# The first pair's maxima in another order, its small work moved to GpSimd, fillers that go on until the first score, and a re-planned order

## The chip, the cores and the metric

The kernel runs on one core of a Trainium2 chip. The metric is device microseconds of one execution; a lower time is better. One execution is also recorded by the hardware profiler, and the rows below come from that one. Engines are named as in the profile: PE (matmuls), PEld (its weight loads), DVE (VectorE), ACT (ScalarE), POOL (GpSimd) and SP (the queue that issues most transfers).

## The reference

Pooled attention, then a feed-forward layer with a two-slope activation:

```python
q_pool = q.reshape(B, H, S // 2, 2, D).mean(axis=3)       # B 4, H 8, S 1152, D 64
scores = (1 / sqrt(D)) * q_pool @ k.T
scores = scores - scores.max(axis=-1)
attn = exp(scores) / (exp(scores).sum(axis=-1) + 1e-9)
x = (attn @ v)  # laid out as 2304 tokens x 512
h = x @ w_in                                              # 512 -> 2048
y = (max(h, 0) + alpha * min(h, 0)) @ w_out               # 2048 -> 512
```

The scores need more precision than one float32r product gives, so q and k are each split into a high part (a rounded copy, `q1`, `k1`) and a low part (the rest, `q2`, `k2`), and a score is the sum of three products. The weights come as 64-bit floats and are converted and split on the core.

## The kernel before, in words

The 32 heads are worked in 16 **pairs**; a pair's two heads sit in the two 64-row halves of PE, and two matmuls on different halves can run side by side. For a pair there are 576 pooled queries and 1152 keys.

- **Maxima.** Before the scores, each query's maximum is found from a rough product of the high parts (lines 815 and 822, one matmul of 384 columns per query tile, third of the keys and head; 28 results a pair, the last 64 queries apart as "rests"). DVE reduces each from its PSUM bank to one column of `bx` (line 836). The columns are then turned into a row `mq`. For pairs 1 to 15 that is one turn (lines 845, 852) and small transfers; for the first pair it is two turns (`first_turn`, lines 892, 904, 915, 921).
- **Scores.** A group of eight matmuls (line 948) makes the scores of 128 keys for half of the queries (288), for both heads: the last two subtract `mq`. ACT takes the exponential into a tile `pa` (line 964). There are 9 groups in a half of a pair, so 18 groups in a pair.
- **Sums over keys.** The `pa` tiles of a half are added up to two partial sums (line 977), seven adds in a half, some on DVE and some on POOL (the table `ADDS`). PE adds up the partitions (line 1013), four matmuls for each partial sum. Weighted values come from 18 matmuls at the end of a half (line 991).
- **Feed-forward.** The first 5 of 16 blocks of the hidden layer are done in "low sweeps", the rest in "high sweeps" after attention (line 477). The weights' conversion (lines 404 to 425 and 386, 389) goes in between on ACT and DVE.

The order on each engine is written by a planner: a list scheduler (`Scheduler`) has a duration, a priority and the buffers of each task and places tasks as its plan says; each engine then runs its list in that order, and waits where an input is late. `lock=True` marks tasks that the planner keeps from overlapping between DVE and POOL. Parameters such as `TO_PE`, `M0` or `W0` shift priorities and assumed delays.

At the start `warm` issues filler matmuls (line 1123) on two otherwise unused banks, while loads and the first reduces go on. `first_prep` loads the first pair in pieces, sums the two halves of each query pair (line 740), and makes the low parts (lines 770 and 781).

Of the kernel before, what the change touches and what calls it, by code (L numbers as in the profile page):

```python
# [225 lines left out]
def attention_ffn(  # L226
# [11 lines left out]
    DF: int = 1843,  # L238
    D0: int = 1153.836,
    AQ: int = 0,  # L240
    F0: float = 6.733,
    F2: float = 0.839,
    FD: tuple = (0, 0, 0),
    WE: float = 13.725,
    WG: int = 1,
    WT: float = 9.076,
    WM: int = 2,
    WB: int = 300,
    WN: int = 4,
    TO_PE: int = 127,  # L250
    FROM_PE: int = 0,
    SLP: int = 47,
    SLA: int = 48,
    SLD: int = 108,
    QL: float = -0.025,
    KL: float = 1.207,
    KR: float = 1.483,
    KS: float = 0.198,
    M0: float = 0.994,
# [7 lines left out]
    KKB: int = 2,  # L267
    SF: int = -39,
    Q0: float = -3.222,
# [5 lines left out]
    ADDS: tuple = ((4, 6, 8), (6, 7, 8)),  # L275
# [5 lines left out]
    R0: float = 6.346,  # L281
    R1: float = -5.36,
    R2: float = -5.985,
    R3: float = -0.231,
    W0: float = 5.682,
    W1: float = 3.256,
    W2: float = 23.45,
    W3: float = 0.87,
# [5 lines left out]
    GL: float = 21.701,  # L294
    COL: float = 0.135,
    HW: float = -1.196,
# [407 lines left out]
    first_load = [None]  # L704

    def first_prep():
# [4 lines left out]
        qc = (slice(0, 2 * P), slice(2 * P, 3 * P), slice(3 * P, SQ))  # L711
# [24 lines left out]
        for i, c in enumerate(qc):  # L736
            m = c.stop - c.start
            q_sum.append(add(
                DVE, dve(m),
                lambda c=c: nc.vector.tensor_tensor(  # L740
# [19 lines left out]
            ACT, act(D), lambda: nc.scalar.activation(out=w.rt.t[:, D:2 * D], in_=qs.t[:, REM:], func=AF.Copy),  # L760
            uses=[qs], deps=[q_sum[2]], writes=[w.rt], prio=-8.3,
# [27 lines left out]
    def pair_max(n, w):  # L789
# [11 lines left out]
        items[BD:BD] = rests  # L801
        if first:
            items = [(t, j) for t in range(NQT - 1) for j in range(NJ)] + rests
        items = [(t, j, i) for t, j in items for i in range(2)]
        for x, (t, j, i) in enumerate(items):
# [7 lines left out]
            def rows(t=t, j=j, d=d, ms=ms):  # L813
                if t >= 0:
                    nc.tensor.matmul(  # L815
                        out=ms.t[:, :JW], lhsT=w.q1.t[d, t * P:(t + 1) * P],
                        rhs=w.k1.t[d, j * JW:(j + 1) * JW], start=True, stop=True,
                    )
                    return
# [7 lines left out]
            dur = 140 if rest else 95  # L827
            if first:
                deps = w.k_in if rest else [w.k_in[j], w.q_in[(0, 0, 1, 2)[t]]]
# [9 lines left out]
            if first and x in (6 * NJ - 1, len(items) - 1):  # L839
                first_turn(x > 6 * NJ, w, bx, mx, mq)  # L840
# [43 lines left out]
    def first_turn(h, w, bx, mx, mq):  # L884
        ts = ((0, 1, 2), (3, -1))[h]
        p = -8.8 + 0.1 * h
        m = Buf(r_one)

        def peak(lo, n):
            return add(  # L890
                DVE, 90,
                lambda: nc.vector.tensor_reduce(
                    out=mx.t[:, lo:lo + n], in_=bx.t[:, lo:lo + n], axis=AX.X, op=ALU.max
                ),
                reads=[bx], deps=list(mx.writers), writes=[mx], prio=p,
            )

        done = [peak(2, 3), peak(6, 3)] if not h else [peak(0, 2 * NQT)]

        def turn():  # L900
            for x, t in enumerate(ts):
                for i in range(2):
                    col = i if t < 0 else 2 + t + i * (NQT - 1)
                    nc.tensor.matmul(
                        out=m.t[i * D:i * D + 1, x * P:(x + 1) * P], lhsT=mx.t[:, col:col + 1].bitcast(F32),
# [3 lines left out]
        add(PE, 110 * 2 * len(ts), turn, deps=done, uses=[mx], writes=[m], prio=p, kind="s", col=2)  # L909
        for i in range(2):  # L910
            o = slice(i * D, i * D + 1)
            lo, hi = (0, 3 * P) if not h else (3 * P, 4 * P)
            w.mq_in[h].append(add(
                ACT, act(hi - lo, True),
                lambda o=o, lo=lo, hi=hi: nc.scalar.activation(out=mq.t[o, lo:hi], in_=m.t[o, :hi - lo], func=AF.Copy),
                reads=[m], writes=[mq], prio=p + 0.01 * i,
            ))
            if h:
# [3 lines left out]
                        out=mq.t[o, REM:], in_=m.t[o, P:2 * P].rearrange("o (i q) -> o q i", q=D), axis=AX.X, op=ALU.max  # L922
# [305 lines left out]
```

## Time and profile before

| | us |
|---|---|
| median of 3 runs | 849.56 (849.19 to 850.66) |
| the profiled execution | 848.91 |
| its span, first to last instruction | 847.1 |
| PE busy in it | 833.1 (98%) |
| DVE busy | 574.5 (68%) |
| ACT busy | 436.4 (52%) |
| POOL busy | 207.3 (24%) |

The profiled execution is 0.65 us under the median, and 1.8 us of it lie outside the span. A busy PE is not PE at its peak: matmuls are pipelined, their ends are modelled, and two halves can run side by side or not. Shares over the whole span mix a stage with attention (to about 430 us) and one of feed-forward alone.

### The profile page before, as it was taken

Reading aid. Unit: us, or ns where it says so; the run is one execution under the profiler, and the core shown is the slowest. Engines: PE = TensorE matmul, PEld = TensorE weight load, DVE = VectorE, ACT = ScalarE, POOL = GpSimd, SP = SyncE. Lnnn points to the kernel's source line nnn. Section 1 sums busy time; section 2 is a strip of 40 time slices with the busy share of each in tenths; the row PEclk is TensorE's granted clock in tenths of the full one; section 3 lists DMA queues with packets and bytes.
Section 4 is the critical chain, followed back from the end, with each engine's and each line's share of the span. In section 5 each row is a group of like instructions: output and inputs, shape, how many; then the busy total and the mean of one; then the engine's idle time right before and its main releaser. Section 6 shows DMA issues by size and latency. Waiting matters only on the chain.

```text
span 847.1 us, 17444 instructions
## 1 busy us (share of the span) xinstructions
PE 833.1 (98%) x6686; PEld 695.8 (82%) x6686; DVE 574.5 (68%) x1071; ACT 436.4 (52%) x1124; POOL 207.3 (24%) x159
## 2 busy tenths in 40 slices
PE   9999999999999999999899999999999999999997
PEld 7776766777777777777679999998888988988986
DVE  7899999999999989888864689733232332322422
ACT  3575756766766766765764567543232143232321
POOL 2353644545555435554420000000000000000000
PEclk9799999999999999999999999999999999999999
DMA  6333444542445433323333766573330321200301
GB/s 218 89 82 114 134 114 127 190 138 76 125 150 143 125 99 87 89 69 99 127 104 110 238 221 224 195 217 88 90 90 0 104 76 45 82 9 1 90 1 45
DMA packets 67759, 93.71 MB, mean 111 GB/s; under 512 B 20004, under 2 KB 45404, under 8 KB 67676
## 3 DMA queue, kind: packets, MB, share of 16 engines
q1 hardware_dynamic: 65516, 88.18, 33.6%
q0 software_dynamic: 2160, 4.42, 3.6%
q8 instruction: 52, 0.85, 0.4%
q14 instruction: 31, 0.25, 0.1%
HBM read 73.48 MB, written 19.02 MB: 109 GB/s over the span
## 4 chain that ended last, share of the span: by engine, by line
PE 88%; DVE 5%; DMA 2%; issue 2%; ACT 2%; SPq 0%; DVEq 0%; ACTq 0%
PE bank L477 43%; PE bank L948 18%; PE bank L991 14%; PE bank L815 6%; PE bank L1013 2%; PE bank L1123 2%; PE bank L822 2%; DMA wraw<-wt 1%; DVE pa L977 1%; DVE bx L836 1%; DVE wbits L413 1%; DMA x<-xs 1%; DVE pos L513 0%; DVE wmag L425 0%; ACT neg L508 0%
## 5 line engine op out<-in xcount | busy, mean ns | idle before, releaser
L977 POOL TENSOR_TENSOR pa<-pa,pa 128x576 f32<-128x576 f32 x128 | 190.6, 1511 | 207.8 <-ACT pa L964 196.5
L836 DVE TENSOR_REDUCE bx<-bank 128x1 f32<-128x384 f32 (+1 forms) x448 | 216.0, 537 | 20.8 <-PE bank L815 14.8
L964 ACT ACTIVATE pa<-bank 128x288 f32<-128x288 f32 x576 | 196.7, 415 | 33.3 <-PE bank L948 23.1
L948 PE MATMUL bank<-q,k 64*128 64x288 f32 x1728 | 207.6, 314 | 0.2
L948 PEld LDWEIGHTS bank<-q,k 64*128 64x128 f32 x1728 | 162.7, 187 | 12.8 <-issue 4.4
L991 PE MATMUL bank<-pa,vv 128*64 128x288 f32 x1152 | 146.8, 409 | 0.0
L991 PEld LDWEIGHTS bank<-pa,vv 128*64 128x64 f32 x1152 | 79.9, 137 | 56.2 <-issue 5.5
L524 DVE TENSOR_TENSOR gw<-gs,gw 128x460 fp32r<-128x460 f32 (+1 forms) x55 | 35.1, 639 | 121.2 <-ACT gw L519 121.2
L948 PE MATMUL bank<-mq,neg 64*128 64x288 f32 x576 | 114.3, 293 | 0.0
L815 PE MATMUL bank<-k,q 64*128 64x384 f32 x384 | 109.4, 366 | 1.9 <-DVE bx L836 1.6
L519 ACT ACTIVATE gw<-gs 128x460 fp32r<-128x460 f32 (+1 forms) x55 | 32.4, 589 | 126.7 <-PE bank L477 115.2
L477 PE MATMUL bank<-wlow,wh 128*128 128x460 f32 (+1 forms) x320 | 92.9, 371 | 0.0
L477 PE MATMUL bank<-gw,wh 128*128 128x460 f32 (+1 forms) x320 | 92.8, 371 | 0.0
L977 DVE TENSOR_TENSOR pa<-pa,pa 128x576 f32<-128x576 f32 x96 | 84.0, 875 | 0.2
L948 PEld LDWEIGHTS bank<-mq,neg 64*128 64x128 f32 x576 | 82.6, 187 | 0.0
L815 PEld LDWEIGHTS bank<-k,q 64*128 64x128 f32 x384 | 62.3, 185 | 16.5 <-DVE bx L836 10.1
L513 DVE SCALAR_TENSOR_TENSOR gs<-gs,nal 128x460 f32<-128x460 f32 (+1 forms) x55 | 38.5, 699 | 52.8 <-ACT gs L508 52.8
L477 PE MATMUL bank<-x,wlow 128*128 128x288 f32 x480 | 66.5, 296 | 0.0
L477 PE MATMUL bank<-gs,wlow 128*128 128x288 f32 x480 | 65.5, 295 | 0.8 <-DVE gs L524 0.7
L477 PEld LDWEIGHTS bank<-wlow,wh 128*128 128x128 f32 x320 | 60.1, 188 | 7.1
L477 PEld LDWEIGHTS bank<-gw,wh 128*128 128x128 f32 x320 | 60.1, 188 | 6.8
L477 PEld LDWEIGHTS bank<-gs,wlow 128*128 128x128 f32 x480 | 63.9, 188 | 1.9 <-DVE gs L524 1.4
(89 smaller groups left out, 996.7 us busy)
## 6 DMA issues: line engine op xcount, KB each, us to landing
wraw<-wt SPq DMA_DIRECT2D x32, 512.0 KB
vv<-vt SPq DMA_DIRECT2D x32, 288.0 KB
xs<-x SPq DMA_DIRECT2D x32, 288.0 KB
x<-xs SPq DMA_DIRECT2D x32, 288.0 KB
kk<-kt SPq DMA_DIRECT2D x15, 576.0 KB
r<-rrd SPq DMA_DIRECT2D x64, 72.0 KB
yp<-ys SPq DMA_DIRECT2D x32, 144.0 KB
wlow<-xs SPq DMA_DIRECT2D x16, 288.0 KB
```

The costliest lines, as they stand in the source:

```text
L477: nc.tensor.matmul(out=ps[:, :n], lhsT=w[a, c // DMO][:, c % DMO:c % DMO + P], rhs=lo(hl), start=(first and i == 0), stop=(last and i == 2),)
L513: lambda: nc.vector.scalar_tensor_tensor(out=flat(pos), in0=flat(neg), scalar=nal[:, f:f + 1], in1=flat(pos), op0=ALU.mult, op1=ALU.add),
L519: ACT, act(n), lambda: nc.scalar.activation(out=gs.t[:, 0, :n], in_=flat(pos), func=AF.Copy),
L524: lambda: nc.vector.tensor_tensor(out=gs.t[:, 1, :n], in0=flat(pos), in1=gs.t[:, 0, :n].bitcast(F32), op=ALU.subtract),
L815: nc.tensor.matmul(out=ms.t[:, :JW], lhsT=w.q1.t[d, t * P:(t + 1) * P], rhs=w.k1.t[d, j * JW:(j + 1) * JW], start=True, stop=True,)
L822: nc.tensor.matmul(out=ms.t[:, :S // 4], lhsT=w.rt.t[d, D - D * u:D - D * u + P], rhs=w.k1.t[d, c:c + S // 4], start=u == 0, stop=u == 1,)
L836: nc.vector.tensor_reduce(out=bx.t[:, at, j:j + 1], in_=ms.t[:, :m], axis=AX.X, op=ALU.max)
L948: nc.tensor.matmul(out=ps.t[i][:, :HQ], lhsT=k.t[d, s] if k else neg[d], rhs=r.t[d, q], start=x == 0, stop=x == len(pairs) - 1,)
L964: lambda ps=ps, p=p, i=i: nc.scalar.activation(out=p.t[:, i], in_=ps.t[i][:, :HQ], func=AF.Exp, scale=SCALE),
L977: lambda a=a, b=p, part=part, e=e: e.tensor_tensor(out=part.t, in0=a.t, in1=b.t, op=ALU.add),
L991: nc.tensor.matmul(out=av.t[i * D:(i + 1) * D, :HQ], lhsT=w.vv[i].t[:, e], rhs=p.t[:, i], start=(e == 0), stop=(e == NC - 1),)
L1013: nc.tensor.matmul(out=ps.t[g * 32:(g + 1) * 32, :HQ], lhsT=ones, rhs=acc[n + g // 2][j].t[:, g % 2], start=j == 0, stop=j == m - 1, tile_ ...
```

## The change

Code: (1) The first pair's maxima come in the order: query tiles 0 and 1, the rests, tiles 2 and 3. For the first pair the rests are queries 256 to 319, so that the first turn covers queries 0 to 319, and so all 288 queries of its first half. (2) `first_turn` takes its bank from the score banks (`r_ps`) in place of bank 0, which the maxima now share from the start. (3) Two of the three query sums, and the three low-part subtractions of the first pair, go to POOL (`FQ`, `FD`). (4) Fillers are planned until the first score group is placed (or 24 us), have 256 columns throughout, and use banks 1 and 7. (5) The planner's assumed times of a maxima matmul (95 to 130 ns, rests 140 to 190 ns), a score group (540 to 545 ns) and a filler are longer. (6) In each half of a pair the add of key tile 7 moves from DVE to POOL (`ADDS`), 32 adds in all. (7) Some 30 priorities and delays of the plan have other values, which moves instructions everywhere.

```diff
-    FD: tuple = (0, 0, 0),
+    FD: tuple = (1, 1, 1),
-    WE: float = 13.725,
+    WE: float = 24.0,
-    WN: int = 4,
+    WN: int = 2,
+    FQ: int = 1,
+    FB: tuple = (1, 7),
-    ADDS: tuple = ((4, 6, 8), (6, 7, 8)),
+    ADDS: tuple = ((4, 6, 8), (6, 8)),
...
-        qc = (slice(0, 2 * P), slice(2 * P, 3 * P), slice(3 * P, SQ))
+        qc = (slice(0, 2 * P), slice(2 * P, 2 * P + D), slice(2 * P + D, SQ))
...
+            eng1, dur, e1 = pair_op(i and FQ, m)
             q_sum.append(add(
-                DVE, dve(m),
-                lambda c=c: nc.vector.tensor_tensor(
+                eng1, dur,
+                lambda c=c, e1=e1: e1.tensor_tensor(
...
-        items[BD:BD] = rests
-        if first:
-            items = [(t, j) for t in range(NQT - 1) for j in range(NJ)] + rests
+        at = 2 * NJ if first else BD
+        items[at:at] = rests
+        starts = [t * P + D * (first and t > 1) for t in range(NQT - 1)]
...
-            dur = 140 if rest else 95
+            dur = 190 if rest else 130
...
-            if first and x in (6 * NJ - 1, len(items) - 1):
-                first_turn(x > 6 * NJ, w, bx, mx, mq)
+            if first and x in (4 * NJ + 3, len(items) - 1):
+                first_turn(x > 4 * NJ + 3, w, bx, mx, mq)
...
-        m = Buf(r_one)
+        m = Buf(r_ps)
...
-        done = [peak(2, 3), peak(6, 3)] if not h else [peak(0, 2 * NQT)]
+        done = [peak(4, 6), peak(8, 10)] if h else [peak(0, 4), peak(6, 8)]
...
-        filler = [Buf(r_av), Buf(r_one)]
+        filler = [Buf(Banks()), Buf(Banks())]
+        for f, i in zip(filler, FB):
+            f.ring.places = [single[i]]
...
-            if sch.now < WE * 1000:
-                add_warm()
+            add_warm()
 
         def add_warm():
-            if not WE:
+            if first_score and first_score[0].end is not None or sch.now > WE * 1000:
                 return
-            n = WN if sch.now < WT * 1000 else WM
-            add(PE, 58 * n, lambda: warm(n), writes=filler, prio=50, kind="warm", col=1)
+            cold = sch.now < WT * 1000
+            n = WN if cold else WM
+            add(PE, (107 if cold else 58) * n, lambda: warm(n), writes=filler, prio=50, kind="warm", col=1)
```

The new file has six more lines, so that its line numbers are 2 to 6 higher (815 becomes 818, 836 becomes 839, 892 becomes 894, 904 becomes 906, 948 becomes 951, 977 becomes 981).

**Place one: PE, from the last maxima of the first pair to its first score.** Before (`k_189`, `q_185` are the first pair's, `k_362`, `q_368` the second's; `rt` holds the rests):

```order
L815 MATMUL bank_118<-k_189,q_185 128x384
L815 MATMUL bank_124<-k_189,q_185 128x384
L822 MATMUL bank_123<-k_189,rt_109 128x288 x2
L822 MATMUL bank_118<-k_189,rt_109 128x288 x2
L822 MATMUL bank_124<-k_189,rt_109 128x288 x2
L822 MATMUL bank_123<-k_189,rt_109 128x288 x2
L904 MATMUL bank_118<-ident,mx_107 1x128 x6
L815 MATMUL bank_124<-k_362,q_368 128x384
L815 MATMUL bank_123<-k_362,q_368 128x384
L904 MATMUL bank_118<-ident,mx_107 1x128 x4
L948 MATMUL bank_119<-q_185,k_189 128x288
L948 MATMUL bank_120<-q_185,k_189 128x288
```

In the changed kernel, at the same place (`k_191`, `q_187` are the first pair's; 1129 is the filler's line):

```order
L818 MATMUL bank_123<-k_191,q_187 128x384
L906 MATMUL bank_120<-ident,mx_107 1x128 x6
L818 MATMUL bank_124<-k_191,q_187 128x384
L818 MATMUL bank_118<-k_191,q_187 128x384
L1129 MATMUL bank_119<-even 128x256
L1129 MATMUL bank_125<-even 128x256
L818 MATMUL bank_123<-k_191,q_187 128x384
L1129 MATMUL bank_119<-even 128x256
L1129 MATMUL bank_125<-even 128x256
L1129 MATMUL bank_119<-even 128x256
L1129 MATMUL bank_125<-even 128x256
L951 MATMUL bank_120<-q_187,k_191 128x288
```

Before, all 28 results of the first pair and both turns stand ahead of the first score. Now 21 of the 28 stand ahead of the first turn and 24 ahead of the first score; the second turn follows four score groups and three maxima of the second pair later. In front of the first maxima matmul stand 36 fillers of 512 columns before, and 38 of 256 columns now.

**Place two: DVE and POOL in the first pair.** DVE before, from the first pair's last reduce on (770 and 781 are the low parts, 892 the step ahead of a turn, 921 the row's last 64 queries):

```order
L836 TENSOR_REDUCE bx_113<-bank_124 128x1
L836 TENSOR_REDUCE bx_113<-bank_123 128x1
L1146 TENSOR_SCALAR nal<-nal 128x16
L892 TENSOR_REDUCE mx_107<-bx_113 128x10
L770 TENSOR_TENSOR q_397<-qs,q_185 128x576
L781 TENSOR_TENSOR k_400<-kk,k_189 128x512
L836 TENSOR_REDUCE bx_114<-bank_124 128x1
L921 TENSOR_REDUCE mq_111<-bank_118 1x64 x2
L836 TENSOR_REDUCE bx_114<-bank_123 128x1
L781 TENSOR_TENSOR k_400<-kk,k_189 128x640
```

DVE in the changed kernel, around the first turn:

```order
L839 TENSOR_REDUCE bx_113<-bank_118 128x1
L894 TENSOR_REDUCE mx_107<-bx_113 128x4
L839 TENSOR_REDUCE bx_113<-bank_123 128x1
L894 TENSOR_REDUCE mx_107<-bx_113 128x2
L839 TENSOR_REDUCE bx_113<-bank_124 128x1
L839 TENSOR_REDUCE bx_113<-bank_118 128x1
L839 TENSOR_REDUCE bx_113<-bank_123 128x1
L923 TENSOR_REDUCE mq_111<-bank_120 1x64 x2
L839 TENSOR_REDUCE bx_113<-bank_124 128x1
```

POOL in the changed kernel, behind its memsets (before, its first two rows there are the transfer of `qs` and the second pair's low part of `k`):

```order
L743 TENSOR_TENSOR qs<-kk 128x64
L743 TENSOR_TENSOR qs<-kk 128x256
L784 TENSOR_TENSOR k_239<-kk,k_191 128x512
L773 TENSOR_TENSOR q_265<-qs,q_187 128x576
L784 TENSOR_TENSOR k_239<-kk,k_191 128x640
L656 DMA qs<-qt 128x576 x2
L699 TENSOR_TENSOR k_431<-kk,k_399 128x1152
L981 TENSOR_TENSOR pa_95<-pa_88,pa_89 128x576
```

The low parts have left DVE's list, and on DVE other reduces now stand behind the steps of the turn. The first mx step comes behind 17 reduces and the second behind 18; 16 of these 18 are those that the first turn needs. From the first reduce to the second pair's mx step (line 845 before, which ends its 28 maxima), DVE's list has 57 reduces both before and now. Apart from the operations above, it has 3 adds of line 977 there before and 2 now, and of a weight tile's conversion line 407 before, and lines 407, 413 and 419 now.

**Place three: DVE near the end of attention, the last adds of pair 14** (counted from 0; lines 407 to 425 and 389 convert weights). Before:

```order
L977 TENSOR_TENSOR pa_103<-pa_103,pa_91 128x576
L413 SCALAR_TENSOR_TENSOR wbits<-wraw,wbits 128x512
L977 TENSOR_TENSOR pa_103<-pa_103,pa_92 128x576
L419 SCALAR_TENSOR_TENSOR wbits<-wraw,wbits 128x512
L407 TENSOR_SCALAR wbits<-wraw 128x512
L425 SCALAR_TENSOR_TENSOR wmag<-wmag,wbits 128x512
L413 SCALAR_TENSOR_TENSOR wbits<-wraw,wbits 128x512
L977 TENSOR_TENSOR pa_103<-pa_103,pa_93 128x576
```

Now:

```order
L981 TENSOR_TENSOR pa_102<-pa_102,pa_91 128x576
L409 TENSOR_SCALAR wbits<-wraw 128x512
L415 SCALAR_TENSOR_TENSOR wbits<-wraw,wbits 128x512
L981 TENSOR_TENSOR pa_102<-pa_102,pa_94 128x576
L421 SCALAR_TENSOR_TENSOR wbits<-wraw,wbits 128x512
```

Between the first and the last of these adds stand one add and five conversion steps before, and two conversion steps now; the middle add is on POOL, and the last one waits for it. On PE the pair's partition sums (line 1013) come after six score groups and twelve feed-forward matmuls before, and after seven groups and twelve such matmuls now.

## Rows read from the trace of the kernel before

**Rows 1.** Stretches: from:to, length, busy (instructions) of PE, PEld, DVE, ACT, POOL, then clock, DMA.

```profile
20.00:25.00 5.00, 4.73 (x23) 2.95 (x23) 4.00 (x11) 0.74 (x2) 0.10 (x1) 0.52 0.00 0
25.00:30.00 5.00, 4.72 (x37) 4.14 (x39) 4.21 (x10) 2.18 (x7) 0.34 (x1) 0.50 0.62 189
150.00:300.00 150.00, 149.83 (x1578) 112.27 (x1575) 144.14 (x283) 101.84 (x284) 75.61 (x54) 1.00 0.45 133
300.00:380.00 80.00, 79.99 (x861) 61.28 (x857) 70.15 (x139) 52.48 (x151) 39.84 (x29) 1.00 0.32 91
```

**Rows 2.** Timeline of PE, four pairs' partition sums: start, duration, instruction.

```profile
160.39 1.18 PE L1013 MATMUL bank<-pa,ones 128*32 128x288 f32 x16
261.93 1.18 PE L1013 MATMUL bank<-pa,ones 128*32 128x288 f32 x16
286.80 1.18 PE L1013 MATMUL bank<-pa,ones 128*32 128x288 f32 x16
386.85 1.18 PE L1013 MATMUL bank<-pa,ones 128*32 128x288 f32 x16
```

**Rows 3.** Timeline of the first pair, all engines.

```profile
1.05 6.93 PE L1123 MATMUL bank<-even 64*128 64x512 f32 x36 [1.05 <-DVE ones L1110]
7.81 0.35 PE L815 MATMUL bank<-k,q 64*128 64x384 f32 x2
8.28 1.02 DVE L836 TENSOR_REDUCE bx<-bank 128x1 f32<-128x384 f32 x2 [3.79 <-PE bank L815]
17.48 2.62 POOL L697 TENSOR_TENSOR k<-kk,k 128x1152 fp32r<-128x1152 f32 x1 [4.45 <-ACT k L682]
26.22 1.09 PE L948 MATMUL bank<-q,k 64*128 64x288 f32 x6
46.50 0.18 DVE L845 TENSOR_REDUCE mx<-bx 128x10 fp32r<-128x30 f32 x1
```

**Rows 4.** Groups of DVE from 8.28 to 46.50 us, and that stretch's busy times.

```profile
L977 DVE TENSOR_TENSOR pa<-pa,pa 128x576 f32<-128x576 f32 x3 | 2.9, 957 | 0.0
L781 DVE TENSOR_TENSOR k<-kk,k 128x512 fp32r<-128x512 f32 (+1 forms) x2 | 1.5, 750 | 0.0
L770 DVE TENSOR_TENSOR q<-qs,q 128x576 fp32r<-128x576 f32 x1 | 0.7, 748 | 0.0
L740 DVE TENSOR_TENSOR qs<-kk 128x128 f32<-128x128 f32 (+1 forms) x2 | 0.6, 316 | 0.0
L921 DVE TENSOR_REDUCE mq<-bank 1x64 fp32r<-1x128 f32 x2 | 0.6, 284 | 0.8 <-ACT mq L915 0.7
L892 DVE TENSOR_REDUCE mx<-bx 128x3 fp32r<-128x9 f32 (+1 forms) x3 | 0.5, 165 | 0.8 <-PE bank L904 0.8
...
8.28:46.50 38.22, 37.23 (x348) 29.51 (x346) 34.67 (x74) 18.34 (x47) 14.08 (x10) 0.87 0.43 128
```

**Rows 5.** Groups of DVE and POOL, 150 to 300 us.

```profile
L836 DVE TENSOR_REDUCE bx<-bank 128x1 f32<-128x384 f32 (+1 forms) x168 | 81.2, 537 | 4.4 <-PE bank L815 2.8 <-PE bank L822 0.3
L413 DVE SCALAR_TENSOR_TENSOR wbits<-wraw,wbits 128x512 int32<-128x512 int32 x5 | 3.4, 681 | 0.0
L977 POOL TENSOR_TENSOR pa<-pa,pa 128x576 f32<-128x576 f32 x48 | 71.0, 1497 | 76.4 <-ACT pa L964 75.4
```

**Rows 6.** Timeline around 420 us, DVE, POOL and PE, and one stretch.

```profile
416.00 0.75 DVE L977 TENSOR_TENSOR pa<-pa,pa 128x576 f32<-128x576 f32 x1
420.51 1.54 POOL L977 TENSOR_TENSOR pa<-pa,pa 128x576 f32<-128x576 f32 x1 [2.48 <-PE bank L1013]
420.71 1.89 DVE L413 SCALAR_TENSOR_TENSOR wbits<-wraw,wbits 128x512 int32<-128x512 int32 x1
422.53 0.75 DVE L977 TENSOR_TENSOR pa<-pa,pa 128x576 f32<-128x576 f32 x1
423.33 1.19 PE L1013 MATMUL bank<-pa,ones 128*32 128x288 f32 x8 [2.96 <-DVE pa L977]
...
422.00:427.00 5.00, 3.67 (x34) 2.75 (x35) 4.96 (x10) 2.54 (x9) 0.06 (x1) 0.66 0.18 71
```

More of the change, by code (lines that the diff above doesn't have):

```diff
@@ L280, in attention_ffn @@
     YSB: int = 4,
-    R0: float = 6.346,
+    R0: float = 4.187,
     R1: float = -5.36,
-    R2: float = -5.985,
+    R2: float = -7.727,
     R3: float = -0.231,
[L285 to L288, printed above, removed]
+    W0: float = 5.34,
+    W1: float = 1.69,
+    W2: float = 18.088,
+    W3: float = 0.137,
     YL: float = 0.337,
@@ L896, in peak @@
             )
[L898 removed]
+        done = [peak(4, 6), peak(8, 10)] if h else [peak(0, 4), peak(6, 8)]
         def turn():
[L901 removed]
+            for x in range(2 + (not h)):
                 for i in range(2):
[L903 removed]
+                    col = i if x == 2 else 2 + 2 * h + x + i * (NQT - 1)
                     nc.tensor.matmul(
[L905 removed]
+                        out=m.t[0][i * D:i * D + 1, x * P:(x + 1) * P], lhsT=mx.t[:, col:col + 1].bitcast(F32),
                         rhs=ident, start=True, stop=True, tile_position=(0, i * D),
                     )
[L909 removed]
+        add(PE, 110 * 2 * (3 - h), turn, deps=done, uses=[mx], writes=[m], prio=p, kind="s", col=2)
+        lo = (2 * P + D) * h
         for i in range(2):
             o = slice(i * D, i * D + 1)
[L912 removed]
             w.mq_in[h].append(add(
[L914 to L915 removed]
+                ACT, act(2 * P, True),
+                lambda o=o: nc.scalar.activation(out=mq.t[o, lo:lo + 2 * P], in_=m.t[0][o, :2 * P], func=AF.Copy),
                 reads=[m], writes=[mq], prio=p + 0.01 * i,
             ))
[L918 removed]
+            if not h:
                 w.mq_in[h].append(add(
@@ L953, in half_main @@
             if n:
-                add(PE, 540, scores, reads=[w.k1, w.q1, w.k2, w.q2, w.mq], writes=[ps], prio=at, kind="s", col=1)
+                add(PE, 545, scores, reads=[w.k1, w.q1, w.k2, w.q2, w.mq], writes=[ps], prio=at, kind="s", col=1)
             else:
-                add(
-                    PE, 540, scores, reads=[w.k1, w.q1, w.q2], uses=[w.k2, w.mq],
+                t = add(
+                    PE, 545, scores, reads=[w.k1, w.q1, w.q2], uses=[w.k2, w.mq],
                     deps=w.k_low[:1 + (c >= 4)] + w.mq_in[0] + (w.mq_in[1] if h else []),
```

51 lines of the change are left out of this document (26 added, 25 removed).

## The prediction

> **What bounds the kernel now.** I read the busy times first, as the table has them: PE is busy 98% of the span, so time can be won only where PE waits, runs at the lower clock, or is less busy than it looks. Then the stretches [rows 1]: from 20 to 30 us the granted clock is 0.52 and 0.50 of full, that is, about 1.2 GHz; from 150 to 380 us it is full and PE has no idle time to speak of.
>
> Which engine sets the pace in the steady part? From 150 to 300 us DVE is busy 144.1 of 150 us (96%), from 300 to 380 us 70.2 of 80 (88%) [rows 1]. The partition sums come once in a pair: from 160.39 to 261.93 is 4 pairs, 25.4 us each, and from 286.80 to 386.85 is 4 pairs, 25.0 us each [rows 2]. With eight points more of room on DVE a pair is 0.37 us (1.5%) shorter. So PE's own stream of matmuls is the bound there, and DVE adds little.
>
> The first pair is another matter [rows 3]. The first maxima matmul starts at 7.81 us, right behind the fillers. The first reduce is at 8.28, the first score at 26.22, and the step that ends the second pair's maxima at 46.50. Of these 38.2 us DVE is busy 34.7 and PE's clock is low for ten [rows 1, 4]: here DVE's list and the clock set the pace, not PE's work. Near 423 us PE waits 2.96 us for one add on DVE [rows 6].
>
> **The start, step by step.** (a) Fillers. 36 of 512 columns, two side by side, take from 1.05 to 7.81 us, 0.376 us a pair of them [rows 3]. Now it is 19 pairs of half the columns: 0.19 us each gives 4.6 us, and up to about 5.5 if all run at the lower clock. The first reduce came 0.47 us behind its matmul; I take 5.9 us for it, 2.4 us sooner than 8.28.
>
> (b) DVE's work until the second pair's mx step. Gone: two query sums (2 x 0.316), two low parts of k (2 x 0.750), one of q (0.748), one add (0.957), together 3.84 us. New: a fourth mx step (0.165) and two conversion steps (0.68 each, line 413's row), together 1.53. Net 2.3 us less [rows 4, 5].
>
> (c) DVE's waits. 38.2 less 34.7 is 3.5 us idle. 0.8 of it was for the turn on PE and 0.8 for the copies of the row on ACT [rows 4]. Both stand now behind other reduces in DVE's list, so I count both as gone; the key's later parts must still land, so that I leave the other 2 us.
>
> The sum is 2.4 + 2.3 + 1.6 = 6.3 us; I take **6.0**, since POOL's sums may come later than DVE's did. The work that hides the moved part: POOL is idle there. Its rows give 2.62 us for 1152 columns [rows 3], 2.3 ns a column; 320 + 512 + 576 + 640 columns are 4.7 us, between the last query load and the first score. Without that cover the first score would wait for the q low part.
>
> Does the PE side allow it? The first turn needs 18 reduces. In the steady part, with three banks, one takes 81.2 / 168 = 0.48 us [rows 5]; 18 of them and two mx steps from 5.9 us are 14.9, and with the turn, its copies and a wait for the later keys the first score comes at 17 to 18 us, 8 to 9 sooner. Nothing gives back the difference to 6.0: PE then waits for DVE, whose list is as in (b). So 9 is the far bound. The near bound is 3: of the 6, three may be lost if PE runs at 1.2 GHz again just behind the first score, as it did before from 20 to 30 us.
>
> **The steady part.** One add in a half goes from DVE to POOL: two a pair, 1.5 us or more less on DVE (0.75 for an undisturbed one [rows 6]), and 2 x 1.50 us more on POOL, which is busy 75.6 of 150 [rows 1, 5]. Pairs with more room on DVE were 0.37 us shorter [rows 2]; over some ten such pairs this is at most 3.7 us. Against it stands what POOL does to DVE. A conversion step that takes 0.68 us on average took 1.89 when it began 0.2 us behind a POOL add of 1.54: it ended about 0.6 us behind that add's end [rows 5, 6]. So such a step is held for up to 1.2 us. The Trainium skill (SBUF — State Buffer, section Who interferes with whom) says that a DVE instruction with two SBUF inputs and a GpSimd instruction that reads SBUF exclude each other for a whole instruction, and that reduces never contend on trn2. These rows agree for the step with two inputs; by that rule every POOL add more is 1.5 us in which no such step can run, and the sum here would tend to zero or a loss. I take a gain of **1.0**; bounds: 3.7 gained, and a loss of 17 (last but one rival). The plan's longer times change no instruction's own length. Mode changes on PE between full-array and half-array work are nearly as many as before; I cost that at nothing.
>
> **The stall near 423 us.** PE's partition sums wait for the last add of pair 14 [rows 6]. Between the first of the last adds, at 416.00, and the last, at 422.53, stood one add and five conversion steps. Now two conversion steps stand there, and the middle add is on POOL: 0.75, then 0.42 to 1.89 us of steps beside a POOL add of 1.5, so about 3 us for the same way in place of 6.5. On PE the sums come one score group later. The wait of 2.96 us goes: **3.0**. What is late next are the conversion steps behind, which PE needs tens of us later. Bounds: nothing (the same add is late for another reason), and 4.7, since the clock was 0.66 of full over 422 to 427 [rows 6], which cost at most another 1.7.
>
> **Sum.** 6.0 + 1.0 + 3.0 = 10.0 us off the profiled execution's 848.91: 838.9. The median of the runs stands 0.65 higher, so the forecast is **839.6**. The stage after attention has the same matmuls and gets nothing; loads keep their sizes.
>
> **Rivals.** They are given against the median of 849.6.
>
> 1. *The clock drops again.* The fillers end at the first score, and then PE waits for reduces between score groups. Before, PE was granted 1.2 GHz from 20 us on, after a stretch with waits of that kind (rows of 4.7 busy of 5 us at 0.52 [rows 1]). Then the start gives 3 and not 6: 842.6. The Trainium skill (TensorE: Matmul & The Clock Gate, section What's actually happening) says that the low clock is the default and activity lifts it; the drop here, with PE busy by its rows, is no proof against that, since those ends are modelled.
>
> 2. *The stall near 420 stays or moves to another add.* The last add now depends on POOL, which has more to do. Then 7 us remain: 842.6 as well.
>
> 3. *Port contention makes DVE the bound (the other side: slower).* A pair has about 1.0 us of idle DVE (5.9 of 150 us over six pairs [rows 1]), and 1.5 to 1.7 more from the adds, together 2.6. A step that POOL holds costs up to 1.2 us [rows 5, 6]. If the longer POOL list holds DVE for more than 2.6 us a pair beyond what it does now, every pair gets longer; from 2.6 + 10 / 14 = 3.3 us a pair on, over some 14 pairs, the whole change is slower. With one held step more than the room, 1.2 x 14 = 17 us are lost: 849.6 - 10 + 17 = 856.6. For it: POOL's share goes from 50% to some 63%. Against it: the reduces, over half of DVE's time, run at 537 ns beside a POOL that is half busy [rows 5].
>
> 4. *The change doesn't bring what it does.* The first score comes sooner, but the second pair's scores don't, because DVE is held up elsewhere and PE waits there: start 1, steady part 0, stall 0: 848.6.
>
> **Chances and range.** Forecast 0.44 (its own range 836 to 842), rival 1 0.20, rival 2 0.16, rival 3 0.10, rival 4 0.10. From 834.5 (far bound of the start with the steady part's and the stall's more than half) to 848 holds the forecast, rivals 1 and 2 and a part of rival 4, about 0.82. A difference under about 0.2% (1.7 us) cannot be told from none in this kernel. Faster by over 0.2% are the forecast, rivals 1 and 2 and a little of rival 4: 0.82; within it most of rival 4: 0.08; slower rival 3: 0.10.
>
> **What would show it.** Start: first reduce at 5.5 to 6.5 us, first score at 17 to 19, second pair's mx step near 40.5, low parts on POOL ended before 16 us. Clock: full in the stretch from 15 to 30 us if rival 1 fails. Steady part: partition sums 25.0 to 25.3 us apart, DVE busy under 93% from 150 to 300 us, POOL near 63%; a distance over 26 us is rival 3. Stall: no wait of PE over 1 us for an add at the end of attention. The prediction is wrong if the second pair starts no sooner, or if the reduces get longer beside POOL.

## The result, and the profile after

The changed kernel takes 840.21 us (median; single runs 839.95 to 842.46), the kernel before 850.11 us on the same chip. The ratio is 0.9889, with an interval of 0.9868 to 0.991: the change is faster by 1.1%. The forecast was 839.6 us. Its sum came close because two errors nearly cancel: the start won more than forecast, and the steady part lost where a gain was forecast. The stall came out as forecast. The rows below show this.

The page of the profile after, with its span, busy times and the clock in 40 slices:

```profile
span 838.2 us, 17447 instructions
...
PE 825.2 (98%) x6690; PEld 691.4 (82%) x6690; DVE 567.0 (68%) x1035; ACT 437.4 (52%) x1124; POOL 262.4 (31%) x196
...
PEclk9999999999999999999999999999999999999999
```

The span is 8.9 us shorter. POOL has 55 us more to do, DVE only 7.5 us less, though 32 adds of about 0.75 us went away. The clock row has no dip.

The same stretches as in [rows 1], and the one of [rows 6]:

```profile
core 0: us, PE busy (x) PEld busy (x) DVE busy (x) ACT busy (x) POOL busy (x), PEclk, DMA share, GB/s
20.00:25.00 5.00, 4.95 (x52) 3.65 (x54) 4.89 (x14) 4.96 (x14) 4.19 (x3) 1.00 0.61 159
25.00:30.00 5.00, 5.00 (x62) 4.58 (x61) 4.84 (x12) 4.19 (x14) 2.80 (x2) 1.00 0.01 6
150.00:300.00 150.00, 148.06 (x1551) 110.65 (x1548) 138.82 (x264) 99.19 (x276) 89.68 (x65) 1.00 0.46 134
422.00:427.00 5.00, 5.00 (x43) 2.84 (x41) 2.55 (x3) 0.00 (x0) 4.92 (x4) 1.00 0.04 2
```

The clock is full where it was 0.52, 0.50 and 0.66. But from 150 to 300 us PE is now idle for 1.94 us, where it was idle for 0.17 [rows 1], with DVE at 92.5%.

The timeline of the first pair, in answer to [rows 3]:

```profile
1.06 4.42 PE L1129 MATMUL bank<-even 64*128 64x256 f32 x38 [1.06 <-DVE ones L1114]
5.28 0.84 PE L818 MATMUL bank<-k,q 64*128 64x384 f32 x3
5.91 1.02 DVE L839 TENSOR_REDUCE bx<-bank 128x1 f32<-128x384 f32 x2 [1.12 <-PE bank L818]
11.60 1.58 POOL L784 TENSOR_TENSOR k<-kk,k 128x640 fp32r<-128x640 f32 x1
15.51 0.82 PE L906 MATMUL bank<-ident,mx 128*1 128x128 f32 x12
17.84 0.67 PE L951 MATMUL bank<-q,k 64*128 64x288 f32 x6 [0.57 <-DVE mq L923]
40.12 0.17 DVE L848 TENSOR_REDUCE mx<-bx 128x10 fp32r<-128x30 f32 x1
```

The start came out as forecast: first reduce at 5.91 (5.9), first score at 17.84 (17 to 18), POOL done with the low parts at 13.18, the second pair's maxima at 40.12 (40.5), 6.4 us sooner than the 46.50 of [rows 3].

To see where the time goes after that, one needs an event that stands at the same place of the work in both kernels. The weighted values at the end of a pair's second half do (line 991 before, 995 after). Timelines of PE, first before, then after, for pairs 0, 3, 7, 13 and 15:

```profile
49.53 2.65 PE L991 MATMUL bank<-pa,vv 128*64 128x288 f32 x20
232.12 3.13 PE L991 MATMUL bank<-pa,vv 128*64 128x288 f32 x24
382.33 2.89 PE L991 MATMUL bank<-pa,vv 128*64 128x288 f32 x22
438.77 2.40 PE L991 MATMUL bank<-pa,vv 128*64 128x288 f32 x18
```

```profile
42.10 3.13 PE L995 MATMUL bank<-pa,vv 128*64 128x288 f32 x24
227.53 2.65 PE L995 MATMUL bank<-pa,vv 128*64 128x288 f32 x20
377.92 3.37 PE L995 MATMUL bank<-pa,vv 128*64 128x288 f32 x26
389.10 1.89 PE L479 MATMUL bank<-x,wlow 128*128 128x288 f32 x12
432.62 3.62 PE L995 MATMUL bank<-pa,vv 128*64 128x288 f32 x28
```

(Pair 3's stand at 129.73 before and at 122.51 after.) The changed kernel is ahead by 7.4 us after the first pair, 7.2 after pair 3, 4.6 after pair 7, 4.4 after pair 13. At the end of attention it is ahead by 6.2, and 18 matmuls of the low sweeps more are done by then (78, before 60); at 0.157 us each (line 479's row) that is 2.8 more, 9.0 in all, close to the 8.9 of the span.

Such a distance counts only where the same work is done ahead of the event. At pair 13 it is not: by a count of the trace's matmuls the changed kernel has 22 more behind it there, two score groups and six matmuls of maxima. The first score of pair 14 is the better event, since the matmuls ahead of it agree within one, fillers apart. Before, then after:

```profile
381.37 0.77 PE L948 MATMUL bank<-q,k 64*128 64x288 f32 x5
```

```profile
375.41 0.29 PE L951 MATMUL bank<-q,k 64*128 64x288 f32 x1
```

There the changed kernel is ahead by 6.0 us. At the first score of pair 4 it is 7.4 (128.21 and 120.78), at that of pair 8 it is 5.0 (230.59 and 225.63); at both it has three short matmuls more behind it. So the start gave 7.4, pairs 4 to 7 took 2.5 back, pairs 8 to 13 gave 1.0, and the end of attention gave 3.0.

### The profile page after: what moved, and what is told of

The parts are those of the page before. It is cut to its first block, busy times and chain, and to the rows that moved or that the text cites. A ratio compares the mean times of both kernels' runs of the same rounds, so it can differ in the third digit from the quotient of the medians.

```text
span 838.2 us, 17447 instructions
## 1 busy us (share of the span) xinstructions
PE 825.2 (98%) x6690; PEld 691.4 (82%) x6690; DVE 567.0 (68%) x1035; ACT 437.4 (52%) x1124; POOL 262.4 (31%) x196
## 4 chain that ended last, share of the span: by engine, by line
PE 86%; DVE 9%; DMA 2%; issue 1%; ACT 1%; SPq 0%; DVEq 0%; ACTq 0%
PE bank L479 44%; PE bank L951 18%; PE bank L995 15%; PE bank L818 6%; DVE bx L839 3%; PE bank L1017 2%; DMA wraw<-wt 1%; DVE x L1066 1%; DVE pa L981 1%; PE bank L825 1%; PE bank L1129 1%; DMA kk<-kt 1%; DVE pos L515 1%; DVE r L1054 0%; DVE wbits L415 0%
## 5 line engine op out<-in xcount | busy, mean ns | idle before, releaser
L981 POOL TENSOR_TENSOR pa<-pa,pa 128x576 f32<-128x576 f32 x160 | 240.5, 1520 | 155.9 <-ACT pa L968 104.4
L839 DVE TENSOR_REDUCE bx<-bank 128x1 f32<-128x384 f32 (+1 forms) x448 | 214.0, 533 | 22.5 <-PE bank L818 19.9
L968 ACT ACTIVATE pa<-bank 128x288 f32<-128x288 f32 x576 | 199.7, 417 | 25.9 <-PE bank L951 17.4
L479 PEld LDWEIGHTS bank<-x,wlow 128*128 128x128 f32 x480 | 64.2, 188 | 1.6 <-issue 1.4
```

Of the source, the lines that this page charges most:

```text
L479: nc.tensor.matmul(out=ps[:, :n], lhsT=w[a, c // DMO][:, c % DMO:c % DMO + P], rhs=lo(hl), start=(first and i == 0), stop=(last and i == 2),)
L839: nc.vector.tensor_reduce(out=bx.t[:, at, j:j + 1], in_=ms.t[:, :m], axis=AX.X, op=ALU.max)
L968: lambda ps=ps, p=p, i=i: nc.scalar.activation(out=p.t[:, i], in_=ps.t[i][:, :HQ], func=AF.Exp, scale=SCALE),
L981: lambda a=a, b=p, part=part, e=e: e.tensor_tensor(out=part.t, in0=a.t, in1=b.t, op=ALU.add),
```

## The experiments

Kernel times are medians. The kernel before took 850.1 to 850.8 us beside them. Unless the text says otherwise, a kernel is the changed one with one edit.

**1. Early fillers long again.**

```diff
         def warm(n):
+            n = 4 if sch.now < WT * 1000 else n
```

> The changed kernel (840.2 us), but the 38 early fillers have 512 columns again in place of 256; the order on every engine is as in the changed kernel. Theory (the end of the fillers sets the first reduce, and the whole start moves with it): first maxima near 7.7 us in place of 5.28, first reduce near 8.3, first score 1.5 to 2.4 us later than 17.84, and all later pairs later by as much: 841.7 to 842.6 us. Rival (the DVE list up to the second pair, with its own waits for loads, sets the second pair's start, and the early end of the fillers is given back there): first score later, second pair's first score within 0.5 us of 46.9, 839.8 to 840.7 us.

Measured: 841.77 us (ratio to before 0.9897, 0.9877 to 0.9917). First reduce at 8.59, first score at 19.9, second pair's first score at 49.0, 2.1 later than after the change; 1.7 of it are left at 406.95, where the last pair's scores begin. The theory holds: the late start is not given back. The times alone would not show it, since the interval overlaps that of the changed kernel (0.9868 to 0.991).

**2. Late fillers left out.**

```diff
-            for f, d in zip(filler, both):
+            for f, d in zip(filler, both) if sch.now < 13725 else ():
```

> The changed kernel, but the fillers that are planned after 13.7 us, between the first pair's last maxima and its first score, are left out; the order is otherwise the same. Theory (the fillers keep the clock at 2.4 GHz over the gaps before the first score): a granted clock near 0.5 of full somewhere in 15 to 30 us, as in the kernel before over 20 to 30 us, and 3 us lost: 842 to 845 us. Rival (the maxima and the turn keep the clock by themselves once they are in the new order): full clock throughout and 839.8 to 840.7 us.

Measured: 840.39 us (0.9887, 0.9865 to 0.9909). First score at 17.6, clock 1.00 in every stretch: a miss for the theory. Planning the fillers until the first score put only eight more into the list, and these do nothing for the clock.

**3. Small operations on VectorE again.**

```diff
             eng1, dur, e1 = pair_op(i and FQ, m)
+            e1 = nc.vector
...
         eng2, dur, e2 = pair_op(FD[0], SQ)
+        e2 = nc.vector
...
             eng3, dur, e3 = pair_op(FD[1 + i], m)
+            e3 = nc.vector
```

> The changed kernel, but the five small operations of the first pair (two query sums, the low part of q, two low parts of k) run on VectorE again, at the places of the plan where they stand now. Theory (DVE's list sets the start, as the prediction has it in step b): 0.3 + 0.4 + 0.6 + 2 x 0.75 us, about 2.9 us more of DVE before the second pair's maxima are turned, the second pair's first score 2 to 3 us later than 46.9 and 842.2 to 843.2 us. Rival (DVE has idle room there that takes them, and PE's own work sets the start): under 1 us, 840.2 to 841.0 us.

Measured: 843.99 us (0.9924, 0.9907 to 0.9941). The second pair's first score stands at 49.8, 2.9 later, just the time of the five steps. The clock was 0.66 from 10 to 15 us here, but DVE has no gap there (5.00 of 5 us busy), so DVE's list sets this delay. A second loss of 2.0 us comes in pair 2. Run 9 shows it too, without these steps, and its rows stand there. Of these 4.9 us, 1.1 are won back in the stage after attention; why is open.

**4. The moved add cut short.**

```diff
-                    lambda a=a, b=p, part=part, e=e: e.tensor_tensor(out=part.t, in0=a.t, in1=b.t, op=ALU.add),
+                    lambda a=a, b=p, part=part, e=e, m=8 if c == 7 else HQ: e.tensor_tensor(
+                        out=part.t[:, :, :m], in0=a.t[:, :, :m], in1=b.t[:, :, :m], op=ALU.add
+                    ),
```

> The changed kernel, but the add of key tile 7 that the change moved to GpSimd covers only 8 of the 288 queries of each head: the instruction stays at its place with its waits, and takes some 0.1 to 0.3 us in place of 1.5, so the sums leave out key tile 7 for most queries. Theory (the longer GpSimd list holds VectorE's steps with two SBUF inputs, and that is why the pairs that convert weights are 26.0 to 26.6 us apart now): those pairs go back to 25.0 to 25.4 us, the mean time of the long two-input steps falls by a third, and 10 to 13 such pairs give 832 to 837 us. Rival (those pairs are bound by PE or by the new order of its matmuls, not by VectorE): distances stay at 26.0 or more, 839 to 841 us.

Measured: 836.16 us (0.9834, 0.9814 to 0.9855), in the range of the theory. From pair 3 to pair 7 (four pairs) the weighted values are 102.5 us apart, where the changed kernel has 105.0 and the kernel before 102.4. Five other runs that keep this part of the list (1, 2, 3, 5 and 9) stay within 0.5 us of the changed kernel there, from the first score of pair 4 to that of pair 8. The order of the instructions is the same in run 4, so PE was not the limit. But only pairs 4 and 5 go back to 25.0 us as the theory has it; pairs 6 and 7 stay at 26.0 and 26.5. The groups of DVE and POOL from 150 to 300 us (count, busy time, mean of one) say what held the changed kernel, beside [rows 5]:

```profile
L839 DVE TENSOR_REDUCE bx<-bank 128x1 f32<-128x384 f32 x143 | 70.6, 547 | 7.4 <-PE bank L818 7.0
L1066 DVE TENSOR_TENSOR x<-r,x 128x288 fp32r<-128x288 f32 x11 | 12.5, 1169 | 0.0
L421 DVE SCALAR_TENSOR_TENSOR wbits<-wraw,wbits 128x512 int32<-128x512 int32 x5 | 4.2, 839 | 0.0
L427 DVE SCALAR_TENSOR_TENSOR wmag<-wmag,wbits 128x512 f32<-128x512 f32 x5 | 4.2, 835 | 0.0
L981 POOL TENSOR_TENSOR pa<-pa,pa 128x576 f32<-128x576 f32 x59 | 86.6, 1480 | 57.8 <-ACT pa L968 42.7 <-DVE pa L981 6.1 <-ACT k L684 3.5
```

In the same stretch of the kernel before, line 1066's step (the low part of x, line 1062 there) has a mean of 542 ns, here 1169. With the add cut short the means fall by a third: from 100 to 280 us this step goes from 1136 to 756 ns, and line 427's from 1009 to 660. One case of the holding, from the timeline of the same kernel:

```profile
137.14 1.72 POOL L981 TENSOR_TENSOR pa<-pa,pa 128x576 f32<-128x576 f32 x1 [1.29 <-DVE pa L981]
137.66 1.76 DVE L427 SCALAR_TENSOR_TENSOR wmag<-wmag,wbits 128x512 f32<-128x512 f32 x1
```

The step with two inputs ends 0.56 us behind the end of POOL's add, about its own undisturbed time (0.68). The reduces keep their 547 ns.

The held time can be added up. Take what each of DVE's instructions lasts beyond the quickest tenth of its kind in all traces of this case, from the first score of pair 4 to that of pair 8: it is 4.6 us before, 10.2 after the change, and 4.0 with the add cut short. A shorter add also ends sooner for whatever needs its sum, which this run does not separate. That part is small, since PE's waits for an add go only from 0.5 to 0.3 us around these pairs.

**5. No filler behind the first maxima.**

```diff
-            for f, d in zip(filler, both):
+            for f, d in zip(filler, both) if sch.now < WT * 1000 else ():
```

> The changed kernel, but only the first 38 fillers are issued, up to the first maxima; none stands between the first pair's maxima, the turn and the scores. The order is otherwise the same. Theory (what keeps the clock at 2.4 GHz is the fillers among the maxima, before 15 us, since leaving out the eight behind them cost nothing): PE busy under 3 of 5 us in 5 to 15 us, granted clock near 0.5 of full over 5 us or more somewhere in 10 to 25 us, first score 1 us or more later than 17.84 and 841.5 to 845 us. Rival (VectorE and the loads set the pace there, and a slow PE is still fast enough): the same drop of the clock, but the second pair's first score within 0.5 us of 46.9 and 839.8 to 841.0 us.

Measured: 841.92 us (0.9895, 0.9879 to 0.9912). Stretches of this kernel:

```profile
5.00:10.00 5.00, 3.00 (x26) 1.89 (x22) 3.09 (x7) 1.76 (x5) 2.02 (x3) 1.00 1.03 384
10.00:15.00 5.00, 4.90 (x15) 3.50 (x15) 4.86 (x11) 1.34 (x2) 3.99 (x4) 0.64 1.06 398
15.00:20.00 5.00, 4.42 (x24) 2.41 (x26) 3.42 (x11) 1.79 (x3) 0.87 (x1) 0.50 0.94 212
20.00:25.00 5.00, 5.00 (x41) 4.49 (x41) 4.32 (x10) 3.63 (x12) 4.72 (x3) 0.50 0.34 98
25.00:30.00 5.00, 4.97 (x57) 4.17 (x55) 5.00 (x12) 4.92 (x14) 1.98 (x2) 1.00 0.10 41
```

PE does 3.00 us of work in 5, then the clock falls to 1.2 GHz and stays there for some 13 us. The first score comes at 19.3, the second pair's at 49.6, 2.7 later. So without the fillers among the maxima, most of which the kernel before had too, the clock is not held. The kernel loses 1.7 us by its median (the intervals overlap) and 2.8 by the span of the profiled execution.

**6. The kernel before with the moved add alone.**

```diff
-    ADDS: tuple = ((4, 6, 8), (6, 7, 8)),
+    ADDS: tuple = ((4, 6, 8), (6, 8)),
```

> The kernel before (850.4 us) with one part of the change: the add of key tile 7 of each half goes to GpSimd, 32 adds, and the planner makes its order anew with that. Theory after the four runs above (each add more on GpSimd holds VectorE's two-input steps, so the steady part gets 0.2 to 0.5 us a pair longer over some eight pairs, and the stall near 423 us goes, 2.96 us and the low clock behind it): 1.6 to 4 us lost, 3 to 4.7 won, 846.5 to 850 us, first score unchanged near 26.2 us. Rival (the prediction's: VectorE's relief is worth 1.0 us in the steady part and the stall 3.0): 845.5 to 846.5 us, pairs of 25.0 to 25.2 us.

Measured: 880.93 us, 3.6% slower (1.0356, 1.0333 to 1.0379). Both expectations missed, by some 30 us. From the first score of pair 4 to that of pair 8 DVE's held time, counted as in run 4, is 23.7 us. Groups of DVE in this kernel from 150 to 300 us, the first answering to [rows 5]:

```profile
L413 DVE SCALAR_TENSOR_TENSOR wbits<-wraw,wbits 128x512 int32<-128x512 int32 x5 | 7.7, 1557 | 0.0
L425 DVE SCALAR_TENSOR_TENSOR wmag<-wmag,wbits 128x512 f32<-128x512 f32 x6 | 6.4, 1066 | 0.0
```

And one place in its timeline, of POOL, DVE and PE:

```profile
42.47 0.88 POOL L654 DMA_DIRECT2D qs<-qt  x1
42.65 4.11 DVE L977 TENSOR_TENSOR pa<-pa,pa 128x576 f32<-128x576 f32 x1
43.08 3.05 POOL L977 TENSOR_TENSOR pa<-pa,pa 128x576 f32<-128x576 f32 x2
47.28 0.68 PE L815 MATMUL bank<-k,q 64*128 64x384 f32 x1 [3.09 <-DVE bx L836]
```

DVE's add is on record from 42.65, but POOL's two adds go ahead of it, and it ends 0.63 us behind them. The reduces behind it in DVE's list are late, so the maxima's banks stay full and PE stands for 3.09 us. This is rival 3 of the prediction, in one row.

**7. The add back on VectorE.**

```diff
-    ADDS: tuple = ((4, 6, 8), (6, 8)),
+    ADDS: tuple = ((4, 6, 8), (6, 7, 8)),
```

> The changed kernel with one part taken back: the add of key tile 7 is on VectorE again in every pair, and the planner makes its order anew. Theory (the start keeps its gain, the pairs that convert weights go back to 25.2 to 25.5 us, and the stall at the end of attention comes back with the add): 2 to 2.5 us won and 3 to 4.7 lost, 840.7 to 843 us; without the stall 837.5 to 838.5. Rival (VectorE's list is the bound, the prediction's reason for a gain in the steady part): pairs longer than 26.0 us and 843 to 848 us.

Measured: 843.61 us (0.9912, 0.9894 to 0.993; single runs 841.39 to 843.81). The time lies in the rival's range, for mixed reasons. Pairs 4 to 7 take 105.0 us together, as in the changed kernel, and two of the four are over 26.0. DVE is busy 102.1 of these 105.0 us with only 5.7 us of held time, so there its own list is the likely bound, as the rival has it. But 2.5 us of the loss are there after the first pair, where a turn came late (the case of run 8, below). PE's longest wait for an add is 1.0 us, so the stall did not come back. At the end of attention PE has two new waits for ACT's exponentials instead, 0.9 and 0.7 us, at 410 and 422.

**8. The add on VectorE in pairs 3 to 9 alone.**

```diff
-                eng, dur, e = (DVE, dve(2 * HQ), nc.vector) if c in ADDS[late_head] else (POOL, 2.4 * 2 * HQ + 50, nc.gpsimd)
+                eng, dur, e = (DVE, dve(2 * HQ), nc.vector) if c in ADDS[late_head] or (c == 7 and 6 <= n < 20) else (POOL, 2.4 * 2 * HQ + 50, nc.gpsimd)
```

> The changed kernel, but the add of key tile 7 is on VectorE in pairs 3 to 9 (those whose VectorE list holds weight conversions and which are 25.5 to 27.5 us long) and on GpSimd in the others; planned anew. Theory (each kind of pair with the less costly place for that add, and no stall at the end): 25.2 to 25.5 us in pairs 3 to 9, 837.5 to 839 us. Rival (what GpSimd holds, VectorE then has to do itself, and nothing is won): 840 to 841.5 us.

Measured: 839.4 us (0.987, 0.9851 to 0.9888; single runs 838.29 to 841.08). This is between the two expectations. The profiled execution is the longest of the four (841.08). Pairs 4 to 7 take 101.7 us in place of 105.0, 25.4 us each, as the theory has it. Run 7 has the add at the same place in these pairs and takes 105.0, so the order around it weighs as much as the engine. 2.6 us are lost at a place where the order is that of the changed kernel. Timeline of POOL, DVE and PE there, and the stretch behind it:

```profile
18.77 2.99 POOL L699 TENSOR_TENSOR k<-kk,k 128x1152 fp32r<-128x1152 f32 x1
20.92 2.23 DVE L1152 TENSOR_SCALAR nal<-nal 128x16 f32<-128x16 f32 x1
21.39 3.21 POOL L981 TENSOR_TENSOR pa<-pa,pa 128x576 f32<-128x576 f32 x2
23.36 0.60 PE L906 MATMUL bank<-ident,mx 128*1 128x128 f32 x8 [1.57 <-DVE mx L894]
```

```profile
25.00:30.00 5.00, 4.97 (x44) 4.52 (x40) 3.93 (x9) 3.42 (x10) 2.10 (x2) 0.66 0.00 0
```

A step on 16 columns, 0.35 us in the changed kernel's profile, takes 2.23 us between POOL's instructions. The second turn is late with it, PE stands, and the clock falls for a time.

**9. That step on ScalarE.**

```diff
-            lambda: nc.vector.tensor_scalar(
-                out=nal, in0=nal, scalar1=-1.0, scalar2=0.0, op0=ALU.mult, op1=ALU.add
-            ),
+            lambda: nc.scalar.activation(out=nal, in_=nal, func=AF.Copy, scale=-1.0),
```

> The changed kernel, but the one small step that negates alpha (128x16, in place) runs on ScalarE at the same place of the plan; nothing else moves. In the profile of the mixed kernel above this step took 2.23 us on VectorE, behind GpSimd's low part of the second pair's k, in the profile of the changed kernel 0.35 us; the turn behind it came 1.7 us later and the clock was 0.66 over 25 to 30 us. Theory (who gets in first there is a matter of a tenth of a us, and makes some executions 2 us slower): the times of single runs lie closer together, all within 839.4 to 840.6 us, median 839.5 to 840.2. Rival (the spread has another cause): single runs up to 842 us as before.

Measured: 842.70 us (0.9907, 0.9887 to 0.9926). The single runs lie close together (842.53 to 843.33), but 2.5 us above the forecast, and none is as short as the rival's: a miss for both. The first pair is as in the changed kernel; 2.0 us are lost in pair 2. Timeline of POOL and DVE at that place, first in the changed kernel, then in this one:

```profile
86.59 0.67 DVE L391 TENSOR_TENSOR wlow<-wmag,wlow 128x512 fp32r<-128x512 f32 x1
86.97 4.78 POOL L981 TENSOR_TENSOR pa<-pa,pa 128x576 f32<-128x576 f32 x1
```

```profile
87.02 2.46 DVE L391 TENSOR_TENSOR wlow<-wmag,wlow 128x512 fp32r<-128x512 f32 x1
87.23 1.70 POOL L981 TENSOR_TENSOR pa<-pa,pa 128x576 f32<-128x576 f32 x1
```

With 0.38 us ahead DVE goes first, and its chain of conversion steps keeps POOL out: the add takes 4.78 us, and no harm is done, since nothing waits for it soon. With 0.21 us ahead DVE loses, and everything behind it is 1.8 us later. In run 3 the same step takes 2.46 us too. The lead alone does not decide it: in run 6 DVE was 0.43 us ahead of POOL's add by the record and lost.

**10. Runs 8 and 9 together.** The edits are those two.

> Both of the last two: the add of key tile 7 on VectorE in pairs 3 to 9 and on GpSimd in the others, and the negation of alpha on ScalarE. Theory: the mixed kernel without the late turn, 1.5 to 2.4 us under its slow executions, 837.0 to 838.5 us, first weighted values near 31.2 us in place of 33.8, full clock throughout. Rival: 839 to 840 us, as the mixed kernel.

Measured: 839.98 us (0.9874, 0.9854 to 0.9893). The first weighted values at 31.2 and the full clock came as expected, pairs 4 to 7 take 101.8 us, but pair 2 loses its 2.0 us as in run 9. So runs 8 and 10 are no measurable gain over the changed kernel's 840.21: each pays at one place what it wins at another.

**11. The planner's times short again.**

```diff
-            dur = 190 if rest else 130
+            dur = 140 if rest else 95
...
-                add(PE, 545, scores, reads=[w.k1, w.q1, w.k2, w.q2, w.mq], writes=[ps], prio=at, kind="s", col=1)
+                add(PE, 540, scores, reads=[w.k1, w.q1, w.k2, w.q2, w.mq], writes=[ps], prio=at, kind="s", col=1)
```

(and the first pair's score groups in the same way)

> The changed kernel with the planner's times of before for a maxima matmul (95 and 140 ns in place of 130 and 190) and a score group (540 in place of 545 ns); no instruction changes, only the order that the planner writes. Theory (the plan keeps GpSimd's adds and VectorE's two-input steps apart in its own time, and only where its times are near the real ones does that hold on the chip): steps with two inputs are held longer, pairs of 26.5 us or more, 845 to 875 us. Rival (the order does not hang on these times): 839 to 842 us.

Measured: 856.75 us, slower than before (1.0067, 1.0045 to 1.009), within the theory's range. The work is the same, the list another. Pairs 4 to 7 take 111.6 us. From 150 to 300 us in this kernel, the stretch and then two groups of DVE:

```profile
150.00:300.00 150.00, 143.81 (x1402) 105.08 (x1404) 134.88 (x248) 93.75 (x257) 86.95 (x59) 0.97 0.45 131
```

```profile
L691 DVE TENSOR_TENSOR q<-qs,q 128x576 fp32r<-128x576 f32 x6 | 5.7, 956 | 0.0
L409 DVE TENSOR_SCALAR wbits<-wraw 128x512 int32<-128x512 int32 x5 | 5.3, 1064 | 0.0
```

PE is idle for 6.2 of 150 us, and steps on DVE that take 0.75 (line 691) and 0.41 (line 409) undisturbed are held. DVE's held time from the first score of pair 4 to that of pair 8 is 13.4 us, 3.2 more than in the changed kernel, and these pairs are 6.7 us longer. So held steps go with the loss; that they make all of it is not shown.

**12. Run 6 with the moved add cut short.** The edit is that of run 4, on run 6's kernel.

> The kernel before with the add of key tile 7 on GpSimd, which took 880.9 us, but that add covers only 8 of the 288 queries of each head, so the sums leave out key tile 7 for most queries; the order is that of the 880.9 us kernel. Theory (there the GpSimd adds hold VectorE's two-input steps, whose means went from 0.68 to 1.07 and 1.56 us, and PE waits for VectorE): most of the 30 us go, 845 to 858 us, and those means fall under 0.85 us. Rival (the order that the planner made there is bad by itself): 868 us or more.

Measured: 862.78 us (1.0154, 1.0123 to 1.0184), between the two. 18 of run 6's 30 us go with the length of the adds. DVE's step of line 425 is back at 695 ns and that of line 413 at 684. 12 us stay. Other steps are still held: DVE's held time from the first score of pair 4 to that of pair 8 is 10.3 us. This run can't tell how much of the 12 us is that and how much the order alone.

## Why the prediction was nearly right

**The start (6.0 forecast, 7.4 found).** At the step that ends the second pair's maxima, for which the sum was worked out, the gain is 6.4. The other 1.0 comes between that step and the weighted values, and no run shows from what. Step (a) was right in its mechanism: run 1 gives back 1.6 of the forecast 2.4 by the medians, and 2.1 at the second pair's first score. Of step (b) run 3 shows the five small steps, at 2.9 us: they count in full, and POOL does hide them. The sum of the steps was 6.3, and I took 0.3 off for POOL's late sums; a clock that stays full had no term in it. Run 5 puts a price of 1.7 to 2.8 us on a low clock here, and in the changed kernel it stayed full. What keeps it up was tested only in part: it isn't the late fillers (run 2); those among the maxima are needed (run 5), but the kernel before had such fillers too, up to 17.6 us, and its clock still fell at 20 us [rows 1]. The new order of the maxima and turns is what is left; it was not run by itself.

**The steady part (1.0 won forecast, 1.5 lost).** This is the step that failed. I weighed DVE's relief against the port and let the relief win, in all pairs alike; the runs show two kinds of pairs. In pairs 4 to 7, where DVE is fullest, 2.5 us are lost: each add more on POOL holds steps with two inputs, and run 4 gives these 2.5 us back by shortening the add alone. In pairs 8 to 13 the change wins 1.0 us (149.8 us, before 150.8, by first scores). Run 7, with the add back on DVE, takes 150.5 there, which speaks for DVE's relief; but the order differs too, so that cause is not shown.

Run 4 prices the add's length on POOL and not the move. With the add on DVE in pairs 4 to 7, run 8 is 3.3 us faster there than the changed kernel and run 7 no faster, so the order has as large a share as the engine.

The Trainium skill (SBUF — State Buffer, section Who interferes with whom) says that a step with two inputs from SBUF and a GpSimd instruction that reads SBUF exclude each other, and that the order of issue decides who waits. These runs agree that either side can be the one held: 1.76 us for L427, 4.78 us for POOL's add. By that rule I had put the sum near zero or at a loss, and for this term that was the better answer.

**The stall (3.0 forecast, 3.0 found).** The wait of [rows 6] is gone, and PE has no wait at all between 395 and 470 us. The low clock behind it is gone too; I had left it out of the term and held it as the bound (0.34 of 5 us, 1.7). Against these stands a smaller wait for an add on DVE, which is new:

```profile
384.22 0.69 PE L1017 MATMUL bank<-pa,ones 128*32 128x288 f32 x8 [1.09 <-DVE pa L981]
```

That much of rival 2 came true. 2.96 and at most 1.7, less 1.1, is at most 3.6, so the size fits, though the 3.0 was reached in part by leaving out two terms of opposite sign. Run 7 has the add on DVE again and no such stall, so the stall goes without the moved add; which part of the order removes it stays open.

**The sum (10.0 forecast, 8.9 found in the span).** That it came this close is in part luck: 1.4 us too little for the start stand against 2.5 too much for the steady part.

**"The plan's longer times change no instruction's own length."** True of the undisturbed lengths, and the cost of nothing that I took from it was the largest mistake in the text, though it doesn't show in the sum. Run 11 shows that these times are worth 16.5 us, and run 6 that the moved add without the new numbers costs 30. The planner keeps POOL's adds and DVE's two-input steps apart in its own time (`lock=True`). Where its times drift from the real ones, the two can meet on the chip; runs 11 and 12 show that this is a part of the cost, not that it is all. Parts (5) to (7) go into one plan, and I priced them as three.

**The rivals.** The clock (rival 1) stayed up. The port (rival 3) is real, at 2.5 us in place of 17 with this plan, and with another plan it makes the kernel slower (run 6). Rival 4 fell with the second pair's start, 6.4 us sooner than before.

## What to carry to other kernels

Where GpSimd and VectorE both read SBUF, price a moved instruction by the steps it can hold, and not only by the busy time that it takes away. Shorten the suspect in place, with the order unchanged, to measure that price; this tells what its length costs there, not what another engine would cost. Treat a scheduler's assumed times as part of the kernel: a move that wins with one set of times can lose several per cent with another, so test an edit together with the times it was planned with. Compare kernels at an event that stands at the same place of the work, and count the work done ahead of it: here 22 matmuls made a gain of 3.0 us look like 4.6.

## What was unexpected of the hardware

- A VectorE step can be passed by more than one instruction of GpSimd: an add that began at 42.65 waited out two adds of together 3.05 us (run 6). GpSimd is kept out in the same way, 4.78 us for an add of 1.4 (run 9's first rows).
- A very small step is held as well: 128x16 elements took 2.23 us in place of 0.35 (run 8). It reads one tile, as line 409's step does (1.06 us in place of 0.41, run 11), so the holding is not confined to steps with two inputs.
- Who goes first can't be told from the recorded starts: DVE 0.38 us ahead won and 0.21 ahead lost (run 9's rows), and 0.43 ahead lost (run 6). A change far upstream moves 2 us in or out (runs 3, 9, 10), so differences of that size between two orders are no proof of a cause.
- The granted clock fell to half after a stretch in which PE had 3.0 of 5 us of work, and stayed low while its record showed 4.4 to 5.0 of 5 (run 5).
